# Attention and a gated MLP on one core: scores of one query block in four computed once instead of twice

## The chip, the cores and the metric

The kernel runs on one core of one Trainium2 chip. The metric is the device time of one execution in microseconds, the median of several runs. The core has five engines, each with its own in-order instruction queue: TensorE (matmul, "PE", with weight loads "PEld"), VectorE ("DVE"), ScalarE ("ACT"), GpSimd ("POOL") and SyncE ("SP"), which here only issues DMAs. Semaphores order work between engines. Matmuls write to PSUM, eight banks of 128 x 512 float32; VectorE and ScalarE read PSUM, GpSimd does not.

## The reference

Two blocks over the same input x (2048 tokens, 448 wide), mixed by a gate per token:

```python
qkv = (x @ wqkv).reshape(B, S, 3, H, Dh)          # H = 16, Dh = 28
scores = jnp.einsum("bhqd,bhkd->bhqk", q, k) * (Dh ** -0.5)
p = softmax(scores, axis=-1)
a = (p @ v) @ wo
gate = x @ W_gate; gate = gate * (gate > 0); up = x @ W_up      # F = 1792
b = (gate * up) @ W_down
g = sigmoid((x * gate_w).sum(-1))
out = g * a + (1 - g) * b
```

All of it is float32.

## The kernel before

Projections, `gu` and the output products run on operands that are split into a high and a low part (`F32R`, a rounded float32), 11 terms to a product of 448 (`TERMS`, L57). High parts are made by a copy (`act_high`, `dve_high`), low parts by a subtraction (`low` on VectorE, `pool_low` on GpSimd).

The order of work is written out by hand. A first phase makes q, k (`qk`, L300) and v (`vproj`). q and k go to DRAM (`qk_d`) and come back one head at a time as 112 rows that hold the four products of high and low parts (`load_k`, `load_q`, L132 to L139); a head is then one matmul deep.

Attention takes scores twice. For the maximum, `smax` (L144) computes queries x keys: one tile has 128 queries and 1024 keys, two matmuls into a double bank `ps_w`, and VectorE reduces it to one column of `mx` (L154). A head has 32 such tiles (`maxima`, L142). `smax_end` (L159) transposes the 2048 maxima, splits them and sends them by DMA into two further rows of Q, against rows of -1 in K. Then `scores` (L173) computes keys x queries: a matmul of 114 rows gives score minus maximum for 128 keys and 512 queries (j, one of `NB` = 4 blocks) in a bank `ps_s`, and ScalarE takes the exponential into a slot P (L180). `pv` (L496) multiplies by V, four 32-row lanes in one bank, and sums of rows come from a column of ones. `row_sums`, `spread` and `normalise` divide by them through DRAM.

32 rounds (`ROUNDS`, L50) go through 16 heads, half a head in each. A round's string is the order on TensorE: `s` one score matmul, `m` one `smax` tile (of a later head), `x` one matmul of the MLP's gate and up product `gu` (`gu_mm`, L462), `h` the last term of two `gu` units as two half-row matmuls. A `gu` unit is 11 matmuls into one bank `ps_x`; ReLU on ScalarE, product on VectorE, the result to DRAM (`spill_h`, L486). FIRST, LONG, WIDE and LATE rounds hold 2, 3, 4 and 4 units. Each round ends with `pv` over its eight key blocks. In DRAM `wgu` has 14 pairs of weight tiles, used once for each of four token blocks: `split_f` splits them anew each time. After attention come the remaining five gate and up pairs, the down product (`down`) and the output product (`wout`).

Of the kernel before, what the change touches and what calls it, by code (L numbers as in the profile page):

```python
# [35 lines left out]
EARLY = (5, 5, 4, 4, 4, 3, 3, 3, 2, 2, 2, 2, 1, 1, 1, 1)  # L36


LEAD = 24

FIRST = "s" * 12 + "mmlssxxxmsxsxuxmsxmsxsxmsxsxmsxsxmsxsxmsxsxmsxsxmsxsxmsx"

LONG = "mxsmsxxxxxsmsxsmsxxsmsxsmsxxsmxxsmsxsxxsmsxxsxsmxsxsmsxxsmsxsmsxxsmsxsxxsmsmxssh"
# [22 lines left out]
def gated_mix_kernel(ctx, tc, x, wq, wo, wgu, wd, out):  # L68
# [73 lines left out]
    maxima = [(h, u, half) for h in range(H) for u in range(NK) for half in range(2)]  # L142

    def smax(k):  # L144
# [5 lines left out]
        for c in range(2):  # L150
            k0 = (half * 2 + c) * TB
            nc.tensor.matmul(ps[:, c, :], Q[h][:GD, u * P:(u + 1) * P], K[h % 3][:GD, k0:k0 + TB],  # L152
                             start=True, stop=True)
        nc.vector.tensor_reduce(MX[h][:, 2 * u + half:2 * u + half + 1], ps, axis=AX.XY, op=OP.max)  # L154
# [656 lines left out]
```

## Time and profile before

| what | us |
|---|---|
| median of 3 runs | 1297.04 (1296.88 to 1297.10) |
| profiled execution, span from first to last instruction | 1294.9 |
| what the median has beside the span | 2.1 |

The profile gives no other time of that execution than its span. Engine busy times are sums over the span. In a group's row, "out<-in" are the program's tile names with partitions x elements, then the count, busy us, the mean ns of one, and the idle time before them with what ended it. A matmul's mean is its latency; the distance between two starts is shorter. A row of the windows view has the stretch, its length, and for each engine busy us and instructions, then the granted clock of TensorE (1.00 throughout), the share of the DMA engines and GB/s. A row of the timeline has start, duration, engine and line.

### The profile page before, as it was taken

To read this page: it belongs to the slowest core of one execution; us is meant where nothing else is said; L and a number is where in the kernel's file an instruction comes from. 1 tells how busy PE (TensorE), PEld (TensorE's weight loads), DVE (VectorE), ACT (ScalarE), POOL (GpSimd) and SP (SyncE) were. 2 spreads that over 40 slices of the span, in tenths; PEclk is the share of its full clock that TensorE was granted. 3 is DMA by queue.
4 is the path that set the end of the run, shared out by engine and by line. 5 is a ranking of instruction groups with operands and counts; after the bars stand their busy time and mean duration, and the time that the engine had idled before them with its cause. 6 is when DMAs were issued, how large, how long until landed. Compare 5 with 4: busy or idle time off the path is not lost.

```text
span 1294.9 us, 17711 instructions
## 1 busy us (share of the span) xinstructions
PE 1289.2 (100%) x6687; PEld 901.0 (70%) x6687; DVE 810.0 (63%) x836; ACT 766.0 (59%) x1400; POOL 367.5 (28%) x551
## 2 busy tenths in 40 slices
PE   9999999999999999999999999999999999999998
PEld 6888766666666666666666666666666656899997
DVE  6487766667677676777766667767677222663342
ACT  5212766666767777777776666767676865322121
POOL 3222132332313222222223322313131354641020
PEclk9999999999999999999999999999999999999999
DMA  9845524151426234141535142423351224644432
GB/s 321 284 160 231 155 75 102 58 125 50 119 59 190 72 84 89 58 102 46 136 104 119 57 104 71 109 67 83 69 144 34 85 82 151 196 135 151 134 110 78
DMA packets 53565, 148.87 MB, mean 115 GB/s; under 512 B 10024, under 2 KB 17128, under 8 KB 48872
## 3 DMA queue, kind: packets, MB, share of 16 engines
q1 hardware_dynamic: 36120, 98.34, 29.2%
q0 software_dynamic: 16928, 48.93, 10.6%
q8 instruction: 53, 0.87, 0.3%
q10 hardware_dynamic: 432, 0.46, 0.1%
q14 instruction: 32, 0.26, 0.1%
HBM read 102.06 MB, written 46.02 MB: 114 GB/s over the span
## 4 chain that ended last, share of the span: by engine, by line
PE 98%; DVE 1%; DMA 0%; SPq 0%; issue 0%; ACT 0%
PE gu L468 22%; PE sm L152 18%; PE po L503 17%; PE s L178 17%; PE acc L712 11%; PE qk L303 5%; PE v L321 3%; PE wo L668 3%; PE s L189 2%; DMA wr<-wq 0%; DVE mx L154 0%; PE mt L162 0%; SPq L253 0%; DVE W L96 0%; DVE y L718 0%
## 5 line engine op out<-in xcount | busy, mean ns | idle before, releaser
L154 DVE TENSOR_REDUCE mx<-sm 128x1 f32<-128x1024 f32 x512 | 614.3, 1221 | 107.8 <-PE sm L152 107.5
L180 ACT ACTIVATE P<-s 128x512 f32<-128x512 f32 x724 | 414.7, 598 | 162.4 <-PE s L178 122.3
L468 PE MATMUL gu<-X,wg 128*128 128x512 f32 (+1 forms) x1232 | 391.5, 401 | 0.0
L178 PE MATMUL s<-Q,K 114*128 114x512 f32 x932 | 368.6, 401 | 0.0
L152 PE MATMUL sm<-K,Q 112*128 112x512 f32 x1024 | 324.1, 398 | 0.1
L468 PEld LDWEIGHTS gu<-X,wg 128*128 128x128 f32 (+1 forms) x1232 | 226.6, 189 | 53.6 <-issue 8.6
L178 PEld LDWEIGHTS s<-Q,K 114*128 114x128 f32 x932 | 175.2, 188 | 88.6 <-ACT P L180 47.5
L152 PEld LDWEIGHTS sm<-K,Q 112*128 112x128 f32 x1024 | 192.1, 190 | 45.7 <-issue 10.1
L503 PE MATMUL po<-P,V 128*32 128x512 f32 x1600 | 181.0, 594 | 0.0
L490 POOL DMA_DIRECT2D h_d<-h x56 | 31.5, 563 | 515.4 <-DVE h L484 469.3
L99 POOL TENSOR_TENSOR wg<-wgr,wg 128x384 fp32r<-128x384 f32 x204 | 146.7, 736 | 8.1
L180 ACT ACTIVATE V<-s 128x512 f32<-128x512 f32 x208 | 119.6, 598 | 42.4 <-PE s L178 30.9
L712 PE MATMUL acc<-WD,hh 128*128 128x448 f32 x672 | 140.9, 368 | 0.0
L712 PEld LDWEIGHTS acc<-WD,hh 128*128 128x128 f32 x672 | 126.2, 188 | 12.8
L503 PEld LDWEIGHTS po<-P,V 128*32 128x32 f32 x1600 | 49.5, 110 | 111.3 <-issue 110.2
L90 ACT ACTIVATE hh<-hr 128x512 fp32r<-128x512 f32 x56 | 35.2, 631 | 119.1 <-PE acc L712 119.1
L96 DVE TENSOR_TENSOR hh<-hr,hh 128x512 fp32r<-128x512 f32 x56 | 46.1, 824 | 64.2 <-ACT hh L90 64.2
L303 PE MATMUL qk<-X,W 128*128 128x512 f32 x308 | 79.5, 397 | 0.4 <-DVE X L96 0.2
L303 PEld LDWEIGHTS qk<-X,W 128*128 128x128 f32 x308 | 57.7, 188 | 15.9 <-DVE X L96 1.3
L90 ACT ACTIVATE wg<-wgr 128x384 fp32r<-128x384 f32 x165 | 66.3, 490 | 2.2 <-PE gu L468 1.2
L509 DVE TENSOR_TENSOR os<-po,os 128x512 f32<-128x512 f32 x16 | 11.1, 692 | 88.7 <-PE po L503 88.7
L96 DVE TENSOR_TENSOR mh<-mr,mh 16x128 fp32r<-16x128 f32 x16 | 5.8, 362 | 88.1 <-ACT mh L166 88.1
(73 smaller groups left out, 758.9 us busy)
## 6 DMA issues: line engine op xcount, KB each, us to landing
wgr<-wgu SPq DMA_DIRECT2D x55, 512.0 KB
K<-qk_d SPq DMA_DIRECT2D x64, 224.0 KB
Q<-qk_d SPq DMA_DIRECT2D x64, 224.0 KB
h_d<-h POOLq DMA_DIRECT2D x56, 256.0 KB, 2.3
hr<-h_d SPq DMA_DIRECT2D x56, 256.0 KB
qk_d<-st POOLq DMA_DIRECT2D x21, 512.0 KB, 3.8
x_d<-X POOLq DMA_DIRECT2D x6, 1024.0 KB, 5.2
X<-x_d SPq DMA_DIRECT2D x24, 256.0 KB
```

The costliest lines, as they stand in the source:

```text
L90: nc.scalar.activation(dst, src, AF.Copy)
L96: nc.vector.tensor_tensor(dst, src, f32(high), op=OP.subtract)
L99: nc.gpsimd.tensor_tensor(dst, src, f32(high), op=OP.subtract)
L152: nc.tensor.matmul(ps[:, c, :], Q[h][:GD, u * P:(u + 1) * P], K[h % 3][:GD, k0:k0 + TB], start=True, stop=True)
L154: nc.vector.tensor_reduce(MX[h][:, 2 * u + half:2 * u + half + 1], ps, axis=AX.XY, op=OP.max)
L178: nc.tensor.matmul(ps, K[h % 3][:GD + 2, kt * P:(kt + 1) * P], Q[h][:GD + 2, j * TB:(j + 1) * TB], start=True, stop=True)
L180: nc.scalar.activation(PT[i][:, j], ps, AF.Exp, scale=SCALE)
L303: nc.tensor.matmul(ps, W[:, a, c * P:(c + 1) * P], xf(tb, b), start=(n == 0), stop=(n == NT - 1))
L321: nc.tensor.matmul(ps[:, :VC], xf(tb, b)[:, t * P:(t + 1) * P], W[:, a, 2 * D:], start=(n == 0), stop=(n == NT - 1))
L468: nc.tensor.matmul(ps, WS[i][rows, s, a], xf(i // NF, b)[rows], start=(n == 0), stop=(n == NT - 1))
L503: nc.tensor.matmul(po[32 * j:32 * j + 32], V[:, h // 4 % 2, i % NK, h % 4], p[:, j], start=(i == i0), stop=(i == i0 + ni - 1))
L712: nc.tensor.matmul(ACC[i // NF][t][:, :D], HH[i][:, a, t * P:(t + 1) * P], WD[:, f, b], start=(f == 0 and n == 0), stop=(f == NF - 1 and n ...
```

## The change

In each head the last block of 512 queries (j = 3; `TQ`, one of four) no longer has its maximum taken by `smax`. `maxima` keeps 24 of 32 tiles a head, and the block's rows of maxima in Q are zero. Its keys x queries scores are copied raw by ScalarE into a slot. `block_max` takes running maxima on VectorE over the half head's eight key blocks, down to 128 x 512. `all_max` reduces that over the partitions on GpSimd (`partition_all_reduce`), `take_max` subtracts it from each slot of 128 x 2048 on GpSimd (letter `g`) or VectorE (`d`), and `take_exp` (`e`) takes one exponential over 2048 in place. As a half head (now called a visit) has its own running maximum, the second half continues from the first, and `rescale` corrects the first half's sums (`c`, `f` on GpSimd; `C`, `F` on VectorE). The other three blocks go as before, two matmuls to a double bank and one eviction of 1024 elements.

Beside that: the two buffers `s` become a third double bank that takes turns with the two of `mx`; `po` uses `ps_x` and is made in two parts, `P` and `Q`; `smax` and scores use all 128 rows of K and Q, so Q gets rows of zeros; the weights of the gate and up product, once split, are stored in DRAM (`ws_d`) and loaded from there for the later token blocks (`load_f`); `h` is gone; small DMAs move from GpSimd's queue to SyncE's; `WO` is split after attention.

```diff
-EARLY = (5, 5, 4, 4, 4, 3, 3, 3, 2, 2, 2, 2, 1, 1, 1, 1)
-LEAD = 24
-FIRST = "s" * 12 + "mmlssxxxmsxsxuxmsxmsxsxmsxsxmsxsxmsxsxmsxsxmsxsxmsxsxmsx"
-LONG = "mxsmsxxxxxsmsxsmsxxsmsxsmsxxsmxxsmsxsxxsmsxxsxsmxsxsmsxxsmsxsmsxxsmsxsxxsmsmxssh"
-WIDE = "sxxmxmxxsxxmsxxsxsmxxssxmxmxsxxsxxsxsmsxxsmxssxxxsmsxxsxmsxmsxsxmsxsmxsxsxxsmsxxsmsmsxxsxsh"
-LATE = "ssxxxssxxxssxxssxx" * 4 + "hh"
-ROUNDS = [(FIRST, 2)] + ([(LONG, 3)] * 2 + [(WIDE, 4)]) * 2 + [(LONG, 3)] * 2
-ROUNDS += ([(WIDE, 4)] + [(LONG, 3)] * 8) * 2 + [(LONG, 3)] * 2 + [(LATE, 4)] * 3
-NP = 9
+TQ = [1] * H
+EARLY = (5, 4, 4, 3, 2, 2, 1, 1)
+AHEAD = 2
+NP = 10
+FIRST = "xxxmxAsmxlsumxxxsmxxsmxsmxsmsmxsgxmdsexxxmexxmsxxmwxPQ"
+LONG = "mmnsxxxsxxxsxxssmxxsxxsxxAmsxxxsmsxxgmxsxmxsxsxcmsxexxmxgmsxfxsexxxmmPwQ"
+WIDE = "msxsxxsxxxsxmnxAxxxsmxxxxssxxxmxxxsxxssxxmxsxxmmxsxgexxmxxgmxxxCsxxsxmxxsmxeFsxmwPQ"
+LATE = "ssnxxsxxxxxxsxsxxxxxssxxxxxxxsxssxxAdxxsxxxxdsxsxexCxsxxxsxxexfxwsxxxPQ"
+ROUNDS = [(FIRST, 2)] + [(WIDE, 4) if k % 7 == 2 else (LONG, 3) for k in range(2 * H - 4)] + [(LATE, 4)] * 3
...
+    banks = ctx.enter_context(ExitStack())
+    third = [banks.enter_context(tc.tile_pool(name="third", bufs=1, space=PSUM))]
+    turns = [None]
+    def next_third(pair):
+        banks.close()
+        third[0] = banks.enter_context(tc.tile_pool(name="third", bufs=1, space=PSUM))
+        turns[0] = 0 if pair else None
     def ps_s(name):
-        return psum.tile([P, TB], F32, tag="s", bufs=2, name=name)
+        return third[0].tile([P, TB], F32, tag="s", bufs=2, name=name)
 
     def ps_w(name):
+        if turns[0] is not None:
+            turns[0] += 1
+            if turns[0] % 3 == 0:
+                return third[0].tile([P, 2, TB], F32, tag="w", bufs=1, name=name)
...
-        Q[h] = q_slot(f"Q_{h}").rearrange("p j t -> p (j t)")
+        Q[h] = QS[h % 3].rearrange("p j t -> p (j t)")
+        if h > 2:
+            nc.sync.dma_start(f32(Q[h])[GD:GD + 2], f32(Q[h])[GD + 2:GD + 4])
...
+    NM = [2 * NK - 8 * n for n in TQ]
+    maxima = [(h, u, half) for h in range(H) for u in range(NM[h] // 2) for half in range(2)]
...
-            nc.gpsimd.dma_start(f32(Q[h])[GD + r:GD + r + 1], f32(mh)[:, r])
-    PT = {}
-    def scores(i, j):
-        h, kt = divmod(i, NK)
-        if j == 0:
-            PT[i] = p_slot(i % NP, f"P_{i}")
-        ps = ps_s(f"s_{i}_{j}")
-        nc.tensor.matmul(ps, K[h % 3][:GD + 2, kt * P:(kt + 1) * P], Q[h][:GD + 2, j * TB:(j + 1) * TB],
-                         start=True, stop=True)
-        nc.scalar.activation(PT[i][:, j], ps, AF.Exp, scale=SCALE)
-    def scores_pair(i, j):
-        h, kt = divmod(i, NK)
-        if j == 0:
-            PT[i] = p_slot(i % NP, f"P_{i}")
-        ps = ps_w(f"s_{i}_{j}")
-        for c in range(2):
-            nc.tensor.matmul(ps[:, c], K[h % 3][:GD + 2, kt * P:(kt + 1) * P], Q[h][:GD + 2, (j + c) * TB:(j + c + 1) * TB],
-                             start=True, stop=True)
-        nc.scalar.activation(PT[i][:, j:j + 2], ps, AF.Exp, scale=SCALE)
...
+            nc.sync.dma_start(f32(Q[h])[GD + r:GD + r + 1], f32(mh)[:, r])
+    AT, QUAD, slots = {}, {}, iter(range(10 ** 6))
+    def visit(v):
+        h, k0 = v // 2, NK // 2 * (v % 2)
+        n, ks = TQ[h], range(k0, k0 + NK // 2)
+        pairs = [((v, j, k // 4), k % 4 // 2, [(k, j), (k + 1, j)]) for j in range(NB - n, NB) for k in ks[::2]]
+        if n == 1:
+            for k in ks[::2]:
+                pairs += [((v, 0, k // 2), c, [(k + c, 0), (k + c, 1)]) for c in range(2)]
+                pairs += [((v, 2, k // 4), k % 4 // 2, [(k, 2), (k + 1, 2)])]
+        else:
+            for k in ks:
+                pairs += [((v, 0, k * (2 - n // 2) // 2), (k if n else j // 2) % 2, [(k, j), (k, j + 1)])
+                          for j in range(0, NB - n, 2)]
+        return [(v, c >= 4 * n, *p) for c, p in enumerate(pairs)]
+    stream = [p for v in range(2 * H) for p in visit(v)]
+    todo_max, todo_sub, todo_exp, todo_all = [], [], [], []
+    RM = {}
+    def block_max(v, j, k, q):
+        n = TQ[v // 2]
+        b = j - NB + n
+        if (v, b) not in RM:
+            if b == 0:
+                rm = att.tile([P, max(TQ), TB], F32, name=f"rm_{v}", tag=f"rm{v % 2}", bufs=1)
+                for c in range(n):
+                    RM[v, c] = rm[:, c]
+        r, p = RM[v, b], QUAD[q]
+        c = k % 4
+        if k % (NK // 2) == 0:
+            if v % 2:
+                nc.vector.tensor_tensor(r, p[:, c], RM[v - 1, b], op=OP.max)
+                nc.vector.tensor_tensor(r, p[:, c + 1], r, op=OP.max)
+            else:
+                nc.vector.tensor_tensor(r, p[:, c], p[:, c + 1], op=OP.max)
+        else:
+            for d in range(2):
+                nc.vector.tensor_tensor(r, p[:, c + d], r, op=OP.max)
+        if k % (NK // 2) == NK // 2 - 2:
+            todo_all.append((v, b, [(v, j, i) for i in (k // 4 - 1, k // 4)]))
+    def all_max():
+        v, b, quads = todo_all.pop(0)
+        nc.gpsimd.partition_all_reduce(RM[v, b], RM[v, b], P, bass_isa.ReduceOp.max)
+        todo_sub.extend((v, b, q) for q in quads)
+    def take_max(engine):
+        v, b, q = todo_sub.pop(0)
+        engine.tensor_tensor(QUAD[q], QUAD[q], RM[v, b].unsqueeze(1).to_broadcast([P, 4, TB]), op=OP.subtract)
+        todo_exp.append(q)
+    def take_exp():
+        q = min(todo_exp, key=lambda q: (q[0], q[2], q[1]))
+        todo_exp.remove(q)
+        q = QUAD[q].rearrange("p c t -> p (c t)")
+        nc.scalar.activation(q, q, AF.Exp, scale=SCALE)
+    def score(late=True):
+        v, done, q, half, chunks = stream.pop(0)
+        h = v // 2
+        if q not in QUAD:
+            QUAD[q] = p_slot(next(slots) % NP, f"P_{v}_{q[1]}_{q[2]}")
+        ps = ps_w(f"s_{v}_{chunks[0][0]}_{chunks[0][1]}")
+        for c, (k, j) in enumerate(chunks):
+            nc.tensor.matmul(ps[:, c], K[h % 3][:, k * P:(k + 1) * P], Q[h][:, j * TB:(j + 1) * TB], start=True, stop=True)
+            AT[v, k, j] = QUAD[q][:, 2 * half + c]
+        dst = QUAD[q][:, 2 * half:2 * half + 2]
+        if done:
+            nc.scalar.activation(dst, ps, AF.Exp, scale=SCALE)
+        else:
+            nc.scalar.activation(dst, ps, AF.Copy)
+            todo_max.append((v, chunks[0][1], chunks[0][0], q))
+        while late and todo_max:
+            block_max(*todo_max.pop(0))
...
+            ws_d[i] = dram.tile([P, 2, 7, P], F32, name=f"ws_d_{i}")
+            nc.sync.dma_start(ws_d[i], f32(w))
+    ws_d = {}
+    def load_f(i):
+        if NF <= i < NB * NF:
+            WS[i] = fe.tile([P, 2, 7, P], F32R, name=f"wg_{i}", tag="wg", bufs=2)
+            nc.sync.dma_start(f32(WS[i]), ws_d[i % NF])
...
+    def rescale(v, part, engine):
+        h = v // 2
+        n = TQ[h]
+        if v % 2 == 0 or n == 0:
+            return
+        rows = slice(32 * (NB - n), P)
+        if part == 0:
+            RS[h] = fe.tile([P, TB], F32, name=f"rs_{h}", tag="rb", bufs=1)
+            for b in range(n):
+                r = slice(32 * (NB - n + b), 32 * (NB - n + b) + 32)
+                engine.tensor_tensor(RS[h][r], RM[v - 1, b][r], RM[v, b][r], op=OP.subtract)
+        else:
+            d = RS.pop(h)[rows]
+            nc.scalar.activation(d, d, AF.Exp, scale=SCALE)
+            engine.tensor_tensor(OS[h][rows], OS[h][rows], d, op=OP.mult)
...
+    def pv(v, part):
+        h, k0 = v // 2, NK // 2 * (v % 2)
+        if part == 0:
+            PO[v] = ps_x(f"po_{v}")
...
+            elif o == "n":
+                if v % 2 and v < 2 * H - 1:
+                    smax_end(v // 2 + 1)
+            elif o == "w":
+                ready = nxt + (ROUNDS[v + 1][1] if v + 1 < len(ROUNDS) else 2)
+                ready = min(ready + ready % 2, 2 * NF)
+                while parts < ready:
+                    split_f(parts // 2, act_high, pool_low, (parts % 2,))
+                    parts += 1
+                    if parts % 2 == 0:
+                        fetch_f(parts // 2 + 1)
+            elif o == "A":
+                all_max()
+            elif o == "d":
+                take_max(nc.vector)
+            elif o == "g":
+                take_max(nc.gpsimd)
+            elif o == "e":
+                take_exp()
+            elif o in "cCfF":
+                rescale(v, "cf".index(o.lower()), nc.gpsimd if o in "cf" else nc.vector)
...
```

More of the change, by code (lines that the diff above doesn't have):

```diff
@@ L353, in gated_mix_kernel @@
         gate = const.tile([P, 2, NK], F32, name="gate")
-        for k in K[:2]:
-            nc.gpsimd.memset(f32(k)[96:128], -1.0)
+        for k in range(2):
+            nc.gpsimd.memset(f32(K[k])[96:128], -1.0)
+            nc.gpsimd.memset(f32(QS[k])[96:128], 0.0)
         for g in range(G):
@@ L435, in gated_mix_kernel @@
     att = stk.enter_context(tc.tile_pool(name="att", bufs=1))
+    next_third(True)
     done = sum(n for _, n in ROUNDS) // 2
-    SECOND = {sum(n for _, n in ROUNDS[:r + 1]) - 1 - 2 * k for r in range(len(ROUNDS))
-              for k in range(ROUNDS[r][0].count("h"))}
-    def lane(k):
-        return slice(64 * k, 64 * k + 64)
+    assert len(ROUNDS) == 2 * H and done <= NB * NF, (len(ROUNDS), done)
     def split_f(i, high, low, part=(0, 1)):
@@ L464, in gu_mm @@
         a, b = (BY_CHUNK if i else HIGH_FIRST)[n]
-        rows = slice(0, P)
-        if n == NT - 1 and 2 * i + s in SECOND | {k - 1 for k in SECOND}:
-            rows = lane(int(2 * i + s in SECOND))
-        nc.tensor.matmul(ps, WS[i][rows, s, a], xf(i // NF, b)[rows], start=(n == 0), stop=(n == NT - 1))
+        nc.tensor.matmul(ps, WS[i][:, s, a], xf(i // NF, b), start=(n == 0), stop=(n == NT - 1))
         c = b % 4
@@ new lines, in gated_mix_kernel @@
+    PO = {}
+    def pv(v, part):
+        h, k0 = v // 2, NK // 2 * (v % 2)
+        if part == 0:
+            PO[v] = ps_x(f"po_{v}")
+        po = PO[v]
+        for k in range(k0 + 4 * part, k0 + 4 * part + 4):
+            for j in range(NB):
+                nc.tensor.matmul(po[32 * j:32 * j + 32], V[:, h // 4 % 2, k, h % 4], AT.pop((v, k, j)), start=(k == k0),
+                                 stop=(k == k0 + NK // 2 - 1))
+        if part == 0:
+            return
+        if v % 2 == 0:
```

162 lines of the change are left out of this document (68 added, 94 removed).

## The prediction

> **What bounds the kernel now.** I read the profile's first part, then the chain of waits, then the windows of single rounds, then the groups by shape, and last the rows of GpSimd.
>
> ```profile
> span 1294.9 us, 17711 instructions
> PE 1289.2 (100%) x6687; PEld 901.0 (70%) x6687; DVE 810.0 (63%) x836; ACT 766.0 (59%) x1400; POOL 367.5 (28%) x551
> by line: PE gu L468 21.9%; PE sm L152 18.4%; PE po L503 17.3%; PE s L178 17.0%; PE acc L712 10.7%; PE qk L303 5.3%; PE v L321 2.8%; PE wo L668 2.8%; PE s L189 1.7%; DMA wr<-wq 0.4%; DVE mx L154 0.4%; PE mt L162 0.2%; SPq L253 0.1%; issue 0.
> L152 PE MATMUL sm<-K,Q 112*128 112x512 f32 x1024 | 324.1, 398 | 0.1
> L503 PE MATMUL po<-P,V 128*32 128x512 f32 x1600 | 181.0, 594 | 0.0
> ```
>
> TensorE is never idle, and 98% of the chain is matmuls in order. So a matmul less is time less, as long as the others keep up. A `sm` matmul takes 18.4% of 1294.9 us over 1024, 0.233 us; its 398 ns in the group is latency, with the next one already running.
>
> ```profile
> 189.65 7.00 PE po L503 x64
> core 0: us, PE busy (x) PEld busy (x) DVE busy (x) ACT busy (x) POOL busy (x), PEclk, DMA share, GB/s
> 189.65:219.67 30.02, 30.02 (x166) 19.13 (x169) 21.10 (x21) 19.91 (x37) 7.30 (x12) 1.00 0.48 107
> 219.67:252.08 32.41, 32.41 (x178) 21.64 (x181) 22.00 (x22) 22.70 (x44) 9.89 (x16) 1.00 0.18 57
> 1009.70:1034.50 24.80, 24.80 (x147) 15.72 (x149) 2.81 (x6) 19.96 (x28) 9.30 (x15) 1.00 0.30 100
> 616.58 0.49 PE L468 MATMUL gu<-X,wg 64*128 64x512 f32 x2
> 617.01 0.64 PE L503 MATMUL po<-P,V 128*32 128x512 f32 x4
> ```
>
> These are a LONG, a WIDE and a LATE round. Each ends in 7.00 us of `po`. A LATE round has 72 full matmuls and two pairs of half-row ones beside it; a pair takes 617.01 - 616.58 = 0.43 us, so one matmul takes (24.80 - 7.00 - 0.86) / 72 = 0.235 us. I use 0.236 below. VectorE is at 21.1 of 30 us, ScalarE at 20, GpSimd at 7.
>
> **What leaves TensorE.** Each head loses 8 of its 32 `sm` tiles: 16 x 8 x 2 = 256 matmuls, at 0.233 us **59.6 us**. The built program agrees (768 `sm`; `s`, `po`, `gu`, `qk` keep their counts). The 34 half-row pairs become 68 full matmuls: 34 x (0.47 - 0.43) = **+1.4 us**. The floor of the span is 1294.9 - 59.6 + 1.4 = 1236.7 us. A new LONG visit is 33 + 32 + 24 = 89 matmuls x 0.236 + 7.0 = 28.0 us; WIDE 30.6; LATE stays at 24.9.
>
> **VectorE and ScalarE, per LONG visit of 28.0 us.**
>
> ```profile
> L154 DVE TENSOR_REDUCE mx<-sm 128x1 f32<-128x1024 f32 x512 | 614.3, 1221 | 107.8 <-PE sm L152 107.5
> L528 DVE TENSOR_TENSOR os<-os,rb 128x512 f32<-128x512 f32 x16 | 11.3, 707 | 5.1 <-DMA rb<-l_d 5.1
> L509 DVE TENSOR_TENSOR os<-po,os 128x512 f32<-128x512 f32 x16 | 11.1, 692 | 88.7 <-PE po L503 88.7
> L180 ACT ACTIVATE P<-s 128x512 f32<-128x512 f32 x724 | 414.7, 598 | 162.4 <-PE s L178 122.3
> L191 ACT ACTIVATE P<-s 128x1024 f32<-128x1024 f32 x38 | 37.6, 1024 | 7.9 <-PE s L189 6.6
> L90 ACT ACTIVATE X<-xr 128x1024 fp32r<-128x1024 f32 x6 | 6.2, 1056 | 4.6 <-DMA xr<-x 4.6
> L90 ACT ACTIVATE X<-xr 128x512 fp32r<-128x512 f32 x4 | 2.5, 620 | 0.2 <-DMA xr<-x 0.2
> PEld s L178 <- ACT P L180: 47.5, 265, 0.2
> ```
>
> VectorE: 12 reduces x 1.22 = 14.7, 7.5 maxima of 128x512 out of SBUF x 0.707 = 5.3, and what it has now beside its 16 reduces, 21.1 - 19.5 = 1.6: 21.6 us, covered. ScalarE: 16 evictions of 1024 x 1.024 = 16.4 in place of 32 x 0.598 = 19.1, and two exponentials over 2048 in SBUF; 512 more elements cost 1.056 - 0.620 = 0.436, so one is 1.056 + 0.872 = 1.93 us and two are 3.9. With the rest that it has now (19.9 - 19.1 = 0.8 in the LONG window, 22.7 - 19.1 = 3.6 in the WIDE one): 21 to 24 us, covered too, but tighter than before. All `sm` and `s` tiles now share a ring of three double banks, where they had four buffers. I charge one wait of 0.2 us a visit, the longest that the row of `PEld s` shows: 32 x 0.2 = **6.4 us**. If the cover is gone, every us of ScalarE above 28 is a us of the visit.
>
> **GpSimd is the part that can turn it.** Per visit it gets one all-reduce over partitions (R), two subtractions of 128x2048 and, every second visit, two operations on 32x512. The built program shows more: the all-reduce and the subtraction stand in different code libraries, so a library reload stands before each all-reduce and another before the first subtraction, 62 in all. The trace of before has one such instruction, for the library in use at the start.
>
> ```profile
> masks.py:199 POOLq MODIFY_POOL_CONFIG  x2: 11/11/11, 0.9 to 0.9; - x2
> 1.02 0.29 POOL masks.py:199 TENSOR_SCALAR_AFFINE_SELECT ident<-ident 128x128 f32<-128x128 f32 x1
> L99 POOL TENSOR_TENSOR wg<-wgr,wg 128x384 fp32r<-128x384 f32 x102 | 100.5, 1007 | 2.5
> L99 POOL TENSOR_TENSOR on<-or,on 128x1024 fp32r<-128x1024 f32 x8 | 19.5, 2439 | 57.4 <-ACT on L90 57.4
> L99 POOL TENSOR_TENSOR WD<-wdr,WD 128x448 fp32r<-128x448 f32 x14 | 19.9, 1422 | 13.6 <-DVE WD L93 13.4
> L490 POOL DMA_DIRECT2D h_d<-h x56 | 31.5, 563 | 515.4 <-DVE h L484 469.3 <-issue 33.3 <-DVE WD L93 7.6
> h_d<-h POOLq DMA_DIRECT2D x56, 256.0 KB, 2.3
> x_d<-X POOLq DMA_DIRECT2D x6, 1024.0 KB, 5.2
> qk_d<-K POOLq DMA_DIRECT2D x6, 512.0 KB, 7.1
> ```
>
> GpSimd takes (2439 - 1007) / 640 = 2.24 ns an element: a subtraction over 2048 is 2.44 + 2.29 = **4.73 us**, a 512-wide operation 1.29 us. R is unseen: at least one pass over 512 (1.3 us), at most seven halvings of 128 partitions, a pass each (9.0 us). I take the geometric middle, 3.4 us, since the ends are a factor of seven apart.
>
> [...]
>
> The price W of one switch: at the start it is about 0.1 us (affine_select starts at 1.02, the reload's two records are at 0.9). That library may have been there already. [...] I take **2.6 us**, a short landing and some issue: the code's size is nowhere in the profile, and the low row is the only one of the same instruction.
>
> What W does is a chain inside the visit. Its third and fourth raw pairs are issued by slot 11, 2.6 us in. VectorE still has `os` (0.69), two reduces (2.44) and four maxima (2.83) to do, so the all-reduce starts at 6.0 and ends at 9.4. First subtraction done at 9.4 + W + 4.73 = 14.1 + W; exponential 16.1 + W; `P`, at slot 89 (21.0 us), waits if W > 4.9. Behind that exponential on ScalarE stands an eviction (1.02) whose bank the last `sm` at 20.5 needs: it waits if W > 3.4. The second subtraction, on odd visits behind a 1.29 us operation, ends at 20.1 + W, its exponential at 22.1 + W, and `Q` at 24.5 waits if **W > 2.4** (even visits 3.4, by the bank). For 12 odd and 12 even LONG visits that is 12 x (W - 2.4) + 12 x (W - 3.4), terms below zero left out: **2.4 us** at 2.6, nothing at 0.1, 101 us at 7.1. WIDE visits have 2.6 us more before `P`, and LATE ones subtract on VectorE: nothing. In the first visit the split of unit 0's second half stands behind all-reduce and switch: seven maxima (4.9), 3.4, 2.6 and two operations (1.007 and, by the same slope, some 0.6) make 12.5 us, and the matmul that needs it stands at slot 33 (7.8 us): **4.7 us**.
>
> GpSimd's sum is 9.5 + 1.3 + 0.8 for `h_d` (1.5 x 0.563) + 3.4 + 2W = 15.0 + 2W, and 4 us more in the nine visits that split weights: it would bound a 28.0 us visit from W = 6.4 (4.4 there).
>
> **Moved to SyncE's queue.** The DMAs of `mh`, `ls`, `l_d`, `rb` and `o_d` (192) leave GpSimd.
>
> ```profile
> POOL l_d L518 <- DVE rs L517: 91.6, 15, 11.8
> L530 POOL DMA_DIRECT2D o_d<-os x64 | 32.7, 517 | 2.2 <-DVE WD L93 2.2
> L524 POOL DMA_DIRECT2D rb<-l_d x64 | 32.2, 508 | 42.6 <-DMA l_d<-rs 42.4 <-issue 0.2
> ```
>
> That frees GpSimd of half a us for each. On SyncE the weight loads now queue behind such waits, the longest 11.8 us. A load of split weights (0.92 MB, about the 5.2 us of `x_d`) is issued when the buffer's unit ends, and the unit between takes 22 matmuls of a 33-matmul visit, 18 us: 17 us fit, barely. Nothing charged; without that cover `gu` waits for the excess. The tail loses its weight split on ScalarE and VectorE and keeps its matmuls: nothing.
>
> **Sum.** 1236.7 + 6.4 + 2.4 + 4.7 = 1250.2 us of span, and 2.1 us that the median of before (1297.04) lies above its span: **1252 us**, 3.5% faster.
>
> **Rivals.**
> (1) *The switch is a code load*, and takes the place of the removed matmuls. Place: between all-reduce and first subtraction. It decides from W = 4.8, where 12 x 2.4 + 12 x 1.4 + 2.2 more in the first visit use up the gain left without it (1297 - 1250). At W = 6.2, between the landings of 5.2 and 7.1: 79 us in LONG visits, about one in each WIDE one, 8.3 in the first: 1236.7 + 6.4 + 79 + 4 + 8.3 + 2.1 = **1336 us**, slower. For it: the program does ask for other code 62 times, and nothing but the slack covers it. Against: 0.1 us in the only record.
> [...]
> (2) *The all-reduce is slow.* At R = 9.0 the chain is 5.6 us later at W = 2.6: 12 x 5.8 + 12 x 4.8 = 127 us in LONG visits and 10.3 in the first: **1382 us**, slower. For it: nothing in the trace bounds it better. Against: GpSimd passes an element in 2.24 ns, and seven of them one after another are the worst order. [...]
> (3) *Subtractions and VectorE get in each other's way.* `WD` at 448 elements takes 1.42 us where 1.007 + 64 x 2.24 ns gives 1.15: a quarter more beside VectorE's work on SBUF. With subtractions of 5.9 us `Q` waits 2.5 us in odd visits (22.1 + 2.6 + 2.3 against 24.5) and 1.2 in even ones: 44 us, **1295 us**, the gain all but gone. Against: beside the reduces out of PSUM the 1007 ns of `wg` shows no such thing.
>
> **How the numbers follow.** Forecast 0.44; rival 3 in part (1268 to 1294) 0.14, in full, within 0.2% of before (about what a measurement of this kernel can tell from no change), 0.04; (1) 0.30; (2) and worse 0.08. So faster 0.58, same 0.04, slower 0.38. The likeliest case alone runs from 1240 (W = 0.1 and no ring waits: 1236.7 + 2.2 + 2.1 = 1241, and a matmul at the LONG window's (30.02 - 7.00 - 0.43) / 95 = 0.238 us takes one more us off) to 1268, where 18 us are lost that it leaves out. For 8 in 10 the range must reach into rival 1, to W = 7.1 (101 + 4 + 9 us, near 1360): **1235 to 1365**.
>
> **What would show it.** 768 `sm` in the chain at about 14%; LONG visits of 28 us from `po` to `po`. GpSimd idle between the all-reduce and the first subtraction is W, the all-reduce's own record R. If rival 1 holds, TensorE is idle before `po` or the last `sm`, released by ScalarE, 2 to 4 us in each LONG visit and hardly in LATE ones. If `gu` waits for a DMA, SyncE's queue was too full. The prediction is wrong if W is above 4.8.

## The result and the profile after

The changed kernel takes 1542.69 us (median of 4 runs, 1536.65 to 1545.13), the kernel before 1297.04. The ratio is 1.1887, with a 95% interval of 1.1863 to 1.1912: 19% slower, where 3.5% faster was predicted, and above the range. These are lines of the page of the profile after (its span, the busy time of each engine, then the busy tenths of TensorE and its granted clock in 40 slices):

```profile
span 1534.9 us, 17075 instructions
PE 1296.2 (84%) x6431; PEld 880.0 (57%) x6431; DVE 899.7 (59%) x939; ACT 772.5 (50%) x894; POOL 523.1 (34%) x327
PE   9997897887877789797978978778879788999998
PEclk9999898998989899898989989899999889999999
```

The 256 matmuls are gone (6431 for 6687), but TensorE is busy for 84% instead of 100%: it is idle for 239 us (6 before), 216 of them in thirty gaps of over 2 us, all but one in the attention part. No other engine is above 59%. Such a picture, no engine full, is a chain of waits from engine to engine. The waits show its links (engine and line that wait <- what they wait for: us in total, times, longest):

```profile
ACT P L248 <- POOL P L241: 182.0, 37, 11.5
POOL P L241 <- issue: 144.6, 20, 9.6
PE sm L169 <- ACT P L264: 122.0, 18, 11.0
```

TensorE's `sm` waits for a bank that ScalarE has not evicted (the raw copy, L264). ScalarE stands at the exponential (L248) until GpSimd has subtracted (L241). And GpSimd waits "for issue": for no other engine and no DMA. The timelines of GpSimd in two neighbouring LONG visits show what that is (start, us, engine, operation; in brackets the idle time before it):

```profile
577.29 1.80 POOL L236 PARTITION_ALL_REDUCE rm<-rm  x1 [10.41 <-DVE rm L230]
586.35 4.62 POOL L241 TENSOR_TENSOR P<-P,rm 128x2048 f32<-128x2048 f32 x1 [7.26 <-issue]
...
611.34 0.59 POOL L566 DMA_DIRECT2D h_d<-h  x1 [12.02 <-DVE h L560]
618.13 1.80 POOL L236 PARTITION_ALL_REDUCE rm<-rm  x1 [6.20 <-ACT rl L557]
627.00 4.48 POOL L241 TENSOR_TENSOR V<-V,rm 128x2048 f32<-128x2048 f32 x1 [7.07 <-issue]
```

In the first, 577.29 + 1.80 = 579.09, and the subtraction starts at 586.35: 7.26 us between two instructions whose data are ready. That gap is the library reload, W of the prediction. The view by line has its records: two short ones (`MODIFY_POOL_CONFIG`, count, then shortest, median and longest in ns, then first and last start in us) where the gap begins, and nothing behind them. The second row is the reload ahead of the second visit's all-reduce:

```profile
L241 POOLq MODIFY_POOL_CONFIG  x2: 98/98/98, 579.0 to 579.1; - x2
L236 POOLq MODIFY_POOL_CONFIG  x2: 42/42/42, 612.2 to 612.2; - x2
```

The changed kernel has 62 such pairs beside the one at the start. The gap isn't a rest of the all-reduce that the record leaves out. In the LATE visits VectorE's subtraction, which needs the all-reduce's result, starts directly behind that record (in the one below 0.04 us after 1286.05 + 1.80), and the last all-reduce, with no operation of the other library since the one before, starts without a gap behind the DMA issue ahead of it:

```profile
1286.05 1.80 POOL L236 PARTITION_ALL_REDUCE rm<-rm  x1 [6.70 <-issue]
1287.89 4.49 DVE L241 TENSOR_TENSOR P<-P,rm 128x2048 f32<-128x2048 f32 x2 [9.40 <-POOL rm L236]
1313.11 1.74 POOL L236 PARTITION_ALL_REDUCE rm<-rm  x1
```

The second of the LONG visits has another reload ahead of that gap. The all-reduce's own reload stands in the queue behind the spill of a hidden tile (`h_d`, 611.34), and so it begins 8.9 us into the visit, and the all-reduce 14.9 us in, where the first visit has 577.29 - 570.98 = 6.3. The windows of the two visits, from `po` to `po` (length, busy time of each engine, granted clock, DMA):

```profile
core 0: us, PE busy (x) PEld busy (x) DVE busy (x) ACT busy (x) POOL busy (x), PEclk, DMA share, GB/s
570.98:603.24 32.26, 30.00 (x159) 18.47 (x155) 24.23 (x21) 22.00 (x24) 14.55 (x6) 0.95 0.11 38
603.24:644.39 41.15, 30.56 (x157) 18.40 (x154) 23.97 (x26) 19.72 (x19) 12.22 (x6) 0.88 0.44 113
634.39:639.57 5.18, 5.18 (x24) 1.50 (x27) 4.96 (x6) 2.77 (x2) 1.58 (x1) 0.52 0.00 0
```

The two visits take 32.3 and 41.2 us, where the prediction had 28.0 for each. The last row is what follows the longer gap, and TensorE's timeline shows it matmul by matmul:

```profile
634.39 1.22 PE L169 MATMUL sm<-K,Q 128*128 128x512 f32 x2 [10.59 <-ACT P L264]
635.54 1.07 PE L601 MATMUL po<-P,V 128*32 128x512 f32 x3
636.40 1.07 PE L601 MATMUL po<-P,V 128*32 128x512 f32 x3
639.57 0.60 PE L601 MATMUL po<-P,V 128*32 128x512 f32 x3
```

After 10.59 us of idleness the clock is at half: four `po` matmuls take 636.40 - 635.54 = 0.86 us, twice the 0.44 of full clock (7.00 us for 64 in the kernel before). In the whole run TensorE is busy for 117 us at half clock, which costs about half of that, 58 us.

The visits fall into classes by what stands ahead of a reload in GpSimd's queue (lengths from `po` to `po`; the base is the prediction's length without waits):

| visits | count | mean us | base | loss, us |
|---|---|---|---|---|
| LONG, all-reduce at 6.0 to 6.3 us | 9 | 31.8 | 28.0 | 34 |
| LONG, weight splits ahead (4, 6, 8) | 3 | 36.8 | 28.0 | 26 |
| LONG that begin with the second half of a unit: `h_d` ahead, all-reduce at 14.6 to 16.8 | 12 | 41.5 | 28.0 | 162 |
| WIDE, `h_d` ahead of the second reload | 4 | 39.8 | 30.6 | 37 |
| LATE | 3 | 30.8 | 24.9 | 18 |

With the first visit, which ends 14.7 us later than before, and 3 us in the tail, 1236.7 + 277 + 18 = 1532 us, against a span of 1534.9. The losses hold the half clock.

### The profile page after: what moved, and what is told of

It is laid out like the page before. It is cut to its first block, busy times and chain, and to the rows that moved or that the text cites. A ratio compares the mean times of both kernels' runs of the same rounds, so it can differ in the third digit from the quotient of the medians.

```text
span 1534.9 us, 17075 instructions
## 1 busy us (share of the span) xinstructions
PE 1296.2 (84%) x6431; PEld 880.0 (57%) x6431; DVE 899.7 (59%) x939; ACT 772.5 (50%) x894; POOL 523.1 (34%) x327
## 3 DMA queue, kind: packets, MB, share of 16 engines
q1 hardware_dynamic: 49388, 136.32, 30.5%
## 5 line engine op out<-in xcount | busy, mean ns | idle before, releaser
L171 DVE TENSOR_REDUCE mx<-sm 128x1 f32<-128x1024 f32 x384 | 461.7, 1221 | 177.2 <-PE sm L169 176.9
L169 PE MATMUL sm<-K,Q 128*128 128x512 f32 x768 | 254.3, 419 | 172.9 <-ACT P L264 122.0
L547 PE MATMUL gu<-X,wg 128*128 128x512 f32 x1232 | 381.3, 400 | 17.4 <-POOL wg L112 11.6
L258 PE MATMUL s<-Q,K 128*128 128x512 f32 x1024 | 321.1, 401 | 25.2 <-ACT P L262 21.5
L262 ACT ACTIVATE P<-s 128x1024 f32<-128x1024 f32 x306 | 299.3, 1026 | 44.6 <-PE s L258 40.2
L169 PEld LDWEIGHTS sm<-K,Q 128*128 128x128 f32 x768 | 139.9, 196 | 244.1 <-ACT P L264 129.9
L547 PEld LDWEIGHTS gu<-X,wg 128*128 128x128 f32 x1232 | 233.7, 190 | 76.1 <-POOL wg L112 12.0
L241 POOL TENSOR_TENSOR P<-P,rm 128x2048 f32<-128x2048 f32 x45 | 204.0, 4537 | 159.9 <-issue 144.6
L258 PEld LDWEIGHTS s<-Q,K 128*128 128x128 f32 x1024 | 184.6, 190 | 87.6 <-ACT P L262 28.9
L248 ACT ACTIVATE P<-P 128x2048 f32<-128x2048 f32 x52 | 99.4, 1911 | 203.0 <-POOL P L241 182.0
L264 ACT ACTIVATE P<-s 128x1024 f32<-128x1024 f32 x104 | 104.5, 1019 | 75.3 <-PE s L258 73.0
L601 PE MATMUL po<-V 128*32 128x512 f32 x408 | 136.1, 673 | 0.6 <-ACT V L248 0.6
L262 ACT ACTIVATE V<-s 128x1024 f32<-128x1024 f32 x78 | 77.2, 1026 | 24.7 <-PE s L258 24.0
```

The costliest lines, as they stand in the source:

```text
L169: nc.tensor.matmul(ps[:, c, :], Q[h][:, u * P:(u + 1) * P], K[h % 3][:, k0:k0 + TB], start=True, stop=True)
L241: engine.tensor_tensor(QUAD[q], QUAD[q], RM[v, b].unsqueeze(1).to_broadcast([P, 4, TB]), op=OP.subtract)
L248: nc.scalar.activation(q, q, AF.Exp, scale=SCALE)
L258: nc.tensor.matmul(ps[:, c], K[h % 3][:, k * P:(k + 1) * P], Q[h][:, j * TB:(j + 1) * TB], start=True, stop=True)
L262: nc.scalar.activation(dst, ps, AF.Exp, scale=SCALE)
L264: nc.scalar.activation(dst, ps, AF.Copy)
```

## The experiments

Theory A: the reloads cost the time, by where they stand in a queue. Theory B: GpSimd's own work does, through the chain or through SBUF. Theory C: another part of the change. The kernel before took 1295 to 1297 us beside each run. Of the strings with the order the excerpts below show mostly LONG; the others were changed in the same sense.

**One library.** The all-reduce is replaced with an operation of the subtraction's library, so no reload is left; the kernel then leaves out the reduction over the partitions.

```diff
-        nc.gpsimd.partition_all_reduce(RM[v, b], RM[v, b], P, bass_isa.ReduceOp.max)
+        nc.gpsimd.tensor_tensor(RM[v, b], RM[v, b], RM[v, b], op=OP.subtract)
```

> The changed kernel with one edit: the all-reduce over partitions is replaced by a GpSimd subtraction of the same 128x512 tile from itself, which stands in the library already loaded, so no reload is left; it leaves out the reduction over partitions (zero is subtracted from the scores in its place). Theory A (the loss is the reloads, 7.1 to 7.3 us each in the trace, and the TensorE clock that falls behind the stalls): 1240 to 1270 us, GpSimd goes from that operation to the first subtraction without a gap, no half clock in the records. Theory B (GpSimd's own work on the chain, two subtractions of 4.5 us and VectorE held up beside them, is too long for a visit): still above 1400 us. Theory C (another part of the change costs the time: shared ring, paired scores, weights out of DRAM, SyncE's queue): above 1350 us.

1257.89 us, ratio 0.9713 [0.9693, 0.9733]. Page, windows of two LONG visits, and GpSimd's timeline in the first of them:

```profile
PE 1229.1 (98%) x6431; PEld 865.1 (69%) x6431; DVE 861.3 (69%) x939; ACT 769.1 (61%) x894; POOL 497.1 (40%) x327
...
888.22:916.17 27.95, 27.95 (x154) 18.03 (x154) 22.55 (x26) 19.49 (x19) 11.50 (x6) 1.00 0.70 184
916.17:944.17 28.00, 28.00 (x156) 18.21 (x155) 22.86 (x21) 21.90 (x24) 13.74 (x6) 1.00 0.28 105
...
896.22 0.58 POOL L566 DMA_DIRECT2D h_d<-h  x1 [11.97 <-DVE h L560]
896.87 1.03 POOL L236 TENSOR_TENSOR rm<-rm 128x512 f32<-128x512 f32 x1
897.98 9.22 POOL L241 TENSOR_TENSOR P<-P,rm 128x2048 f32<-128x2048 f32 x2
```

These are visits of 28.0 us at full clock, with both subtractions on GpSimd and no gap ahead of them. In the first, `h_d` stands ahead as in the changed kernel, and without a reload behind it that costs nothing. So 285 us of the changed kernel hang on the reloads. (The substitute takes 1.04 us where the all-reduce takes 1.80; over 32 visits that is 24 us at most.) Theories B and C are left with the 6 us between this time and the predicted 1252.

**VectorE subtracts.** GpSimd keeps the all-reduce alone, and reloads only where it splits weights, in the first nine visits.

```diff
-LONG = "mmnsxxxsxxxsxxssmxxsxxsxxAmsxxxsmsxxgmxsxmxsxsxcmsxexxmxgmsxfxsexxxmmPwQ"
+LONG = "mmnsxxxsAxxxsxxssmxxsxxsxxmsxxxsmsxxdmxsxmxsxsxCmsxexxmxdmsxFxsexxxmmPwQ"
```

> The changed kernel with the subtractions and the rescaling on VectorE in all visits, the all-reduce right behind the last raw pair, and in the first visit behind the weight split. Reloads stay only in the nine visits that split weights on GpSimd, and there off the chain. Theory A: 1245 to 1300 us; VectorE has 12 x 1.22 + 7.5 x 0.75 + 2 x 2.29 + 2.3 = 27 of 28 us, so visits of 28 to 30 us, in the early ones up to 33. Theory B: similar, 1250 to 1300, since GpSimd's subtractions are gone too. Theory C: above 1350 us.

1411.4 us, ratio 1.091 [1.0889, 1.093]: a miss. One of its late LONG visits, without any reload, and the waits:

```profile
1023.92:1054.81 30.89, 28.47 (x154) 18.00 (x154) 26.74 (x28) 19.73 (x19) 2.98 (x4) 1.00 0.75 210
...
PE sm L169 <- DVE mx L171: 38.8, 21, 5.7
PE s L258 <- DVE mx L171: 37.9, 25, 3.3
```

VectorE is busy for 26.7 of 30.9 us, and TensorE now waits for its reduces. I read it so: a subtraction of 2.28 us in VectorE's queue holds up the maxima behind it, and with them the ring of three. The profiled execution is 155 us longer than that of the run before; 68 us of them lie in the first nine visits, which still reload, and 79 in the LONG and WIDE ones behind them, which don't. So the subtraction costs where it goes, too.

**Order of GpSimd's queue.** Same work and same number of reloads; the all-reduce and the first subtraction stand together right behind the last raw pair, ahead of `h_d`.

```diff
-LONG = "mmnsxxxsxxxsxxssmxxsxxsxxAmsxxxsmsxxgmxsxmxsxsxcmsxexxmxgmsxfxsexxxmmPwQ"
+LONG = "mmnsxxxsAgxxxsxxssmxxsxxsxxmsxxxsmsxxmxsxmxsxsxcmsxexxmxgmsxfxsexxxmmPwQ"
```

> The changed kernel with the all-reduce and the first subtraction moved together to right behind the visit's last raw pair, in LONG and WIDE visits: GpSimd's spill of h no longer stands ahead of a reload. All work and all 62 reloads stay. Theory A, with the queue's order as its second half: the LONG visits of 41 us fall to some 32 and the WIDE ones of 40 to 33 or 34, 12 x 9 + 4 x 6 and some clock: 1370 to 1420 us. Theory A without the order (only the reload between all-reduce and subtraction matters): no change, 1530 to 1555. Theories B and C: no change, 1530 to 1555 us.

1412.2 us (2 runs), ratio 1.0905 [1.0884, 1.0927]. 130 us come from the order alone. Outside the visits with weight splits, the all-reduce now starts at 5.3 to 6.4 us in every visit up to the LATE ones. The second of the visits shown above takes 30.7 us now; its window and GpSimd's timeline in it:

```profile
559.64:590.34 30.70, 28.45 (x154) 18.70 (x153) 23.79 (x24) 19.70 (x19) 12.34 (x6) 1.00 0.57 147
...
565.83 1.80 POOL L236 PARTITION_ALL_REDUCE rm<-rm  x1 [10.05 <-ACT P L262]
574.90 4.61 POOL L241 TENSOR_TENSOR V<-V,rm 128x2048 f32<-128x2048 f32 x1 [7.27 <-issue]
579.46 0.74 POOL L566 DMA_DIRECT2D h_d<-h  x1
```

The reload of 7.27 us is still there; what is gone is the wait ahead of the all-reduce.

**No block taken once.** `TQ` is 0: all scores are taken twice, with the change's other parts kept.

```diff
-TQ = [1] * H
+TQ = [0] * H
```

> The changed kernel with no block taken raw (TQ = 0): maxima of all 32 tiles a head by TensorE and VectorE as before, four more of them in each visit's order, no all-reduce, no subtraction, no rescaling. What is left of the change is the paired scores, the ring of three, the weights out of DRAM, the moved DMAs and new orders. Theory A: these cost little, 1290 to 1310 us. Theory B: the same. Theory C: well above 1310 us, by what the other parts cost.

1347.23 us, ratio 1.0404 [1.0389, 1.042]: a miss, and inconclusive. TensorE is at 98%, but a LONG visit takes 31.5 us against 30.0 before, and the largest waits for data at the weight loads are for the ring:

```profile
PEld s L258 <- DVE mx L171: 47.7, 101, 0.8
```

Sixteen `sm` tiles a visit in strings written for twelve wait for VectorE often and briefly. That is the order that I gave it, not proof of a fault in the other parts, which reach 28.0 us in the run with one library. A kernel that keeps these parts without the new block wasn't tuned.

**Mixed.** GpSimd takes the second tile only, VectorE the first while GpSimd reloads; the rescale is VectorE's.

```diff
-LONG = "mmnsxxxsxxxsxxssmxxsxxsxxAmsxxxsmsxxgmxsxmxsxsxcmsxexxmxgmsxfxsexxxmmPwQ"
+LONG = "mmnsxxxsAgxxxsxxssmxxsxxsxxmsdxxxsmsxxmexsxmxsxsxCmsxxxmxmsxFsxxxxemmwPQ"
-        v, b, q = todo_sub.pop(0)
+        v, b, q = todo_sub.pop(-1 if engine is nc.gpsimd else 0)
```

> Nothing is left out. Both reloads of each visit stay, but their places in GpSimd's queue are chosen so that other work covers them: the all-reduce and GpSimd's subtraction stand together right behind the last raw pair; GpSimd takes only the second tile of the block, VectorE takes the first (2.3 us) while GpSimd reloads; the rescale is VectorE's. Theory A (what costs the time is a reload of 7 us that the chain waits for): the first exponential no longer waits for a reload and the second waits for 8.0 + 7.2 + 4.6 = 19.8 us, ahead of the first half of the `pv` matmuls at 20.7; LONG visits of 28 to 29 us, a total of 1255 to 1310 us, the early visits with weight splits keeping up to 40 us of loss. Theory B (GpSimd's own work holds VectorE and the exponentials, with or without reloads): near 1400, as in the run with VectorE's subtractions. If a reload disturbs the other engines even where nothing waits: over 1400.

1354.75 us, ratio 1.0452 [1.0416, 1.0489]: better by 57 us, but over the 1310. The visits mostly alternate between 29.3 and some 32 to 36 us. GpSimd and VectorE in one of the long ones:

```profile
947.71 4.62 POOL L241 TENSOR_TENSOR P<-P,rm 128x2048 f32<-128x2048 f32 x1 [7.05 <-issue]
...
949.97 2.92 DVE L585 TENSOR_TENSOR rs<-rm,rm 32x512 f32<-32x512 f32 x1
952.91 3.49 DVE L171 TENSOR_REDUCE mx<-sm 128x1 f32<-128x1024 f32 x3
```

The rescale's first subtraction (L585, 32x512) takes 2.92 us and ends at 952.89, within 0.6 us of the end of GpSimd's subtraction (952.33). The maxima (L171) start behind it.

**Reloads that nobody waits for.** The kernel before, with an all-reduce and a subtraction of a spare tile in each round.

```diff
+                if ns == 5 * NB:
+                    nc.gpsimd.partition_all_reduce(spare, spare, P, bass_isa.ReduceOp.max)
+                    nc.gpsimd.tensor_tensor(spare, spare, spare, op=OP.subtract)
```

> The kernel before, with one all-reduce and one subtraction of a spare 128x16 tile on GpSimd in the middle of each of its rounds: two reloads a round, 64 in all, that no instruction waits for but the DMA issues of spilled hidden tiles and row sums. Theory A in its narrow form (a reload costs only those who wait for it): 1295 to 1300 us, with two gaps of about 6 to 7.3 us a round in GpSimd's own time. If a reload takes bandwidth, the port or the clock from the others: 1 us or more for each, 1360 us and up.

1348.82 us, ratio 1.042 [1.0382, 1.0459]: neither number. Two neighbouring rounds, GpSimd's timeline in them, and TensorE's wait in the second:

```profile
956.37:986.33 29.96, 29.96 (x163) 19.09 (x163) 22.08 (x22) 21.05 (x39) 5.28 (x11) 1.00 0.72 168
986.33:1026.55 40.22, 32.91 (x163) 21.18 (x163) 20.06 (x18) 21.41 (x40) 13.84 (x23) 0.87 0.17 50
...
985.75 0.39 POOL L602 PARTITION_ALL_REDUCE spare<-spare  x1 [7.86 <-issue]
993.49 0.20 POOL L603 TENSOR_TENSOR spare<-spare 128x16 f32<-128x16 f32 x1 [7.35 <-issue]
994.43 5.91 POOL L100 TENSOR_TENSOR wg<-wgr,wg 128x384 fp32r<-128x384 f32 x8
...
995.49 2.50 PE L469 MATMUL gu<-X,wg 128*128 128x512 f32 x5 [7.31 <-POOL wg L100]
PE gu L469 <- POOL wg L100: 35.0, 14, 7.3
```

The first round holds a reload and takes 29.96 us, as before the change. The second is 10 us longer, because a weight split stood behind the reload and `gu` waited 7.31 us for it; I had forgotten that the kernel before splits weights on GpSimd all the way through. Of the 31 rounds after the first, 17 are within 0.2 us of their length before, three of them with three reloads each; the others pay where someone waits. So a reload as such takes GpSimd's time and, in these rounds, nobody else's, which is theory A. The loss, 50 us in the profiled execution, is 35.0 us of `gu` waiting and the half clock behind it (TensorE is busy for 28 us at half clock, which costs 14).

**The rescale moved.** The mixed kernel with L585 ahead of VectorE's big subtraction, away from GpSimd's.

```diff
-LONG = "mmnsxxxsAgxxxsxxssmxxsxxsxxmsdxxxsmsxxmexsxmxsxsxCmsxxxmxmsxFsxxxxemmwPQ"
+LONG = "mmnsxxxsAgxxxsxxssmxxsxxsxxCmsdxxxsmsxxmexsxmxsxsxmsxxxmxmsxFsxxxxemmwPQ"
```

> The mixed kernel (GpSimd takes the second tile of the block, VectorE the first) with one edit: the first part of the rescale, a subtraction of two 32x512 tiles in SBUF on VectorE, stands ahead of VectorE's big subtraction instead of behind GpSimd's. In the mixed run it took 2.92 us in visit 25 (17.3 to 20.2), until GpSimd's subtraction (15.1 to 19.7) was over, against 0.69 elsewhere, and TensorE then waited 1.69 us for a maximum. If VectorE held by GpSimd is what makes the odd LONG visits 32 to 36 us against 29.3 for the even ones: they come down to 29 to 31 us, 13 of them by some 3 us, a total of 1305 to 1330 us. If something else of the odd visits does it: 1345 to 1360.

1321.86 us, ratio 1.0208 [1.0193, 1.0223], 33 us less. The group of L585 in the mixed run, and then in this one (count, busy us, mean ns):

```profile
L585 DVE TENSOR_TENSOR rs<-rm,rm 32x512 f32<-32x512 f32 x16 | 42.6, 2665 | 0.5
```

```profile
L585 DVE TENSOR_TENSOR rs<-rm,rm 32x512 f32<-32x512 f32 x16 | 11.0, 689 | 6.2 <-POOL rm L236 6.0
```

**Three further places.** The all-reduce of LATE visits ahead of `h_d`, the last rescale on GpSimd so that the library is back before the second stage, and in the first visit the second weight split on VectorE and the all-reduce where the change had it.

```diff
-LATE = "ssnxxsxxxxxxsxsxxxxxssxxxxxxxsxssxxAdxxsxxxxdsxsxexCxsxxxsxxexFxwsxxxPQ"
+LATE = "ssnAxxsxxxxxxsxsxxxxxssxxxxxxxsxssxxdxxsxxxxdsxsxexCxsxxxsxxexFxwsxxxPQ"
-ROUNDS = [(FIRST, 2)] + [(WIDE, 4) if k % 7 == 2 else (LONG, 3) for k in range(2 * H - 4)] + [(LATE, 4)] * 3
+ROUNDS = [(FIRST, 2)] + [(WIDE, 4) if k % 7 == 2 else (LONG, 3) for k in range(2 * H - 4)] + [(LATE, 4)] * 2 + [(LATE.replace("F", "f"), 4)]
-                split_f(0, act_high, pool_low, (1,))
+                split_f(0, act_high, low, (1,))
```

> The same, with the three other places mended at which a reload or GpSimd's queue was waited for in the mixed run: in the last three visits the all-reduce stands ahead of the spilled hidden tile (visit 29 was 34.3 us against 24.9), the last rescale is GpSimd's, so that its library is back before the weight split of the second stage (TensorE waited 8.3 us for it), and the first visit's second weight split is VectorE's and its all-reduce stands where the change had it (that visit ended at 176.6 us against 168.8 in the run without reloads). Theory A: 8 to 9 us less at each of the three, 24 to 26 us under the run before it, 1280 to 1305 us; about level with the kernel before. If these waits are taken up elsewhere: no difference from the run before it, within 5 us.

1303.05 us, ratio 1.0062 [1.0045, 1.0079]: as expected, the best of the kernels that compute everything, and still a little slower than before.

**Four tries at the rest.** Most LONG visits are now at 29.2 to 30.3 us against 28.0. Other orders of VectorE's queue (in the last, `d` and `D` are the two halves of the subtraction):

```diff
-LONG = "mmnsxxxsAgxxxsxxssmxxsxxsxxCmsdxxxsmsxxmexsxmxsxsxmsxxxmxmsxFsxxxxemmwPQ"
+LONG = "mmnsxxxsAgxxxsxxssmxxsxxsxxCmsdxxxssxxsmxxsmexsxxmsxmxxxmsxFmsxxxxemmwPQ"
...
+LONG = "mmnsxxxsAgxxxsxxssmxxsxxsxxCdmsxxxsemsxxmxsxmxsxsxmsxxxmxmsxFsxxxxemmwPQ"
...
+LONG = "mmnsxxxsAgcxxxsxxssmxxsxxsxxdmsxxxsemsxxmxsxmxsxsxmsxxxmxmsxfsxxxxemmwPQ"
...
+LONG = "mmnsxxxsAgxxxsxxssmxxsxxsxxCdmDsxxxsmsxxmexsxmxsxsxmsxxxmxmsxFsxxxxemmwPQ"
```

> The run before it with one edit, in the order of the LONG visits alone: the maxima that stood directly behind VectorE's subtraction (at 10.0, 11.4 and 12.8 us of the visit) and the first exponential stand some 1.4 us later. What is left there (29.2 to 30.3 us a visit against 28.0 in the run without reloads) is put down to VectorE's 2.29 us subtraction, behind which three maxima queue up and hold the ring of score tiles. If that is so: LONG visits near 28.5, 24 of them by about 1 us, 1275 to 1290 us, under the kernel before. If the rest of the loss is GpSimd's subtraction or the weight loads: 1298 to 1306, no change.

> The mended mixed kernel with another order of VectorE's queue in the LONG visits: its big subtraction stands ahead of the maximum at 7.9 us instead of behind it, and the first exponential one pair of scores earlier. The all-reduce is over at 7.8 to 8.0 us, and VectorE stood idle until that maximum at 8.7 to 9.4; the subtraction then ends at about 10.1 to 11.0 us instead of 12.3 to 13.0. If the three maxima behind the subtraction are what holds the ring: LONG visits 0.5 to 1 us shorter, 1280 to 1293 us, under the kernel before. If every place of the subtraction costs the same wait (as moving the maxima later did, which brought 31 us more): 1300 to 1315.

> The same, with both instructions of the LONG visits' rescale back on GpSimd, directly behind its own subtraction, where its library is loaded: no reload more, 1.4 us less for VectorE in each odd visit and some 2.8 us more for GpSimd, after 19.7 us. If VectorE's load sets the odd visits: 5 to 12 us under the run before it. If GpSimd's instructions hold VectorE's maxima of the block at 21 to 25 us by as much: no difference, within 4 us.

> The mended mixed kernel with VectorE's subtraction cut into two of 128x1024 elements (about 1.15 us each), in the LONG visits with one maximum between them, the first half in the gap of VectorE behind the all-reduce. Three orders of this visit have shown 1303, 1320 and 1334 us: wherever the 2.29 us instruction stands, TensorE or ScalarE's exponential waits for it. If its length is what the ring of score tiles can't cover: LONG visits 28.5 to 29 us, a total of 1280 to 1295 us. If it is VectorE's whole load: 1300 to 1310, no change.

1333.89 us (ratio 1.0298 [1.0281, 1.0315]), 1319.61 (1.019 [1.0165, 1.0215]), 1320.29 (1.0191 [1.0176, 1.0206]) and 1316.80 (1.0158 [1.0141, 1.0175]). None comes under the 1303; the first, second and fourth also lie above both numbers that I had given, and the third comes out as no difference from the second. Moved maxima make TensorE wait elsewhere: in the first of the four `sm` waits for VectorE 26.1 us and for ScalarE's exponentials (L262) 16.6, against 5.8 and 1.6 in the run before, while `s` waits for VectorE 8.4 instead of 24.4. In the other three, 8 to 13 of the 14 to 18 us that the profiled execution is longer lie in the eight visits behind the first, in which GpSimd still splits weights, and only 4 to 7 in the twenty behind those; why the early ones pay stays open. Two halves of the subtraction bring no gain either, which speaks against its length by itself as the cause, though in this order they stand close together. How 2.3 us more of VectorE could be covered in these visits stays open.

## Why the prediction was wrong, point by point

**The floor was right.** The sum had 1236.7 us of span and LONG visits of 28.0 us; without reloads the run shows 27.95 and 28.00, and 1257.9 us in all. Ring waits, ScalarE's cover and SyncE's queue, charged at little or nothing, hold there too: its longest wait for loaded weights is 3.1 us, once.

**The failed step: W.** "I take **2.6 us**" was an estimate from the landings of DMAs, and no run shows that term: measured are 7.07 and 7.26 in the visits above and 7.2 on average (144.6 us over the 20 of one group of rows), at and above the 7.1 to which the range reached. Nothing shows W as a landing either: inside the gap of 7.26 us, from 579.1 to 585.7, the profile has no DMA packet of the core. The one record of before, 0.1 us, was no measure of a change. The text itself said that the prediction is wrong above 4.8. Rival 1 thus names the place, the reload as the cause and the point of decision, and its chain holds where its conditions hold: with W = 7.2 and an all-reduce of 1.80 us instead of 3.4, the formula gives 12 odd visits 28.0 + 7.2 - 1.6 - 2.4 = 31.2 us and the even ones 30.2; the nine visits whose all-reduce started on time show 30.5 to 32.7, each 0.3 to 1.6 us more. Its sign shows there too: TensorE is idle for 1.4 to 2.3 us ahead of a late `sm` in each. Ahead of the all-reduce the reload is 6.2 us of idle time on average in the run with the spare tile (198.0 us over 32, at most 7.9). Ahead of a subtraction it is more, 7.2 on average there (144.0 us over 20, at most 8.5) and in the changed kernel (6.8 to 9.6), and it is paid at each change, there and back.

**The missed wait, about half of the miss.** Rival 1 priced all that at 1336 us, near 1360 at its worst, so W alone would have stayed within the range. What took the time beyond it is above all a second wait that no part of the text has. "The all-reduce starts at 6.0" took the reload ahead of the all-reduce for covered. It is, where GpSimd has nothing before it. In the twelve visits that begin with the second half of a `gu` unit, the product of that half ends ahead of the all-reduce's place, and its `h_d` issue stands in front of the reload: the all-reduce starts at 14.6 us or later. The same holds for the second reload in WIDE visits (I had "nothing": 9.2 us each) and the first in LATE ones ("nothing": 18 us in all). The order experiment shows the size: with the same reloads in other places, 130 us less of the 291 by which the prediction was off; the LATE visits' 18 come on top of these.

**Half clock** was in no sum. Of TensorE's thirty gaps of over 2 us, the 25 of 2.26 to 11.6 us are followed by a granted clock of 0.5, the five of 2.07 to 2.21 aren't, but one of 1.95 us is; around the gap of 10.59 us above, the clock is at half from 629 to 639 us. All in all half clock costs about 58 us, which are part of the losses above.

**First visit**: 4.7 us predicted, 14.7 measured, of which 2.2 are left in the run with one library. The rest is the same W, in this timeline of GpSimd, ahead of the weight split:

```profile
145.01 1.80 POOL L236 PARTITION_ALL_REDUCE rm<-rm  x1 [5.94 <-DVE pair L109]
155.33 0.98 POOL L112 TENSOR_TENSOR wg<-pair,wg 128x384 fp32r<-128x384 f32 x1 [7.74 <-issue]
```

**Rival 2** falls, and R was over-sized. The groups of the changed kernel (count, busy us, mean ns):

```profile
L236 POOL PARTITION_ALL_REDUCE rm<-rm x32 | 57.6, 1801 | 230.1 <-DVE rm L230 81.7 <-issue 51.3 <-ACT rl L557 39.4
L241 POOL TENSOR_TENSOR P<-P,rm 128x2048 f32<-128x2048 f32 x45 | 204.0, 4537 | 159.9 <-issue 144.6 <-PE sm L169 14.3
```

1.80 us against 3.4; a subtraction takes 4.54 us against the 4.73 worked out.

**Rival 3** has its mechanism, the other way about: not GpSimd's subtraction becomes slower (4.48 to 4.63 us in the changed kernel), but VectorE's operations on two SBUF tiles (L585 2665 ns in the mixed run, 689 once moved). In the run with one library, where both subtractions are GpSimd's, the visits still take 28.0 us; in the mixed one it costs 33 us.

## What to carry to other kernels

Before GpSimd gets a new operation, list the code libraries of all that it runs, in order: here each change was a gap of some 6 to 7 us in its queue, and a gap costs what waits behind it, so the change belongs right behind the previous instruction, with nothing in front that waits for another engine. When an instruction moves to an in-order queue, write down for every parity of the loop what stands directly ahead of it; one visit that works says nothing of the next. And on VectorE, keep short operations on two SBUF tiles out of the time in which GpSimd works through a large one (here 2665 ns against 689).

## What the runs showed of the hardware

The reload didn't depend on the operand: 7.35 us ahead of a 128x16 subtraction, 7.26 ahead of a 128x2048 one, and 7.2 on average for either. It shows as two records of at most 0.1 us in GpSimd's queue and then as idle time for which the profile names no cause.

VectorE's operations on two SBUF tiles took longer beside GpSimd's large subtraction, some until about its end. In the changed kernel's timeline a 128x512 maximum took 4.25 us (operations of this shape took 707 ns before), while GpSimd subtracted, and ended 0.5 us after it:

```profile
593.09 4.54 POOL L241 TENSOR_TENSOR P<-P,rm 128x2048 f32<-128x2048 f32 x1
...
593.92 4.25 DVE L227 TENSOR_TENSOR rm<-V 128x512 f32<-128x512 f32 x1 [3.18 <-ACT V L264]
```

In the mixed run L585 (32x512) took 2665 ns on average, and 689 ns once it was moved away from GpSimd's subtraction. The reduces out of PSUM (L171) took 1221 ns on average in the changed kernel, as in the kernel before (L154).
